# A planned RWKV-7 + MLP kernel on one core: whole instruction orders compared by four timing cases and a stateful TensorE clock

## Chip, core and metric

The kernel runs on one NeuronCore of one Trainium2 chip. The metric is device time in microseconds (us) of one launch, all inputs and outputs in the chip's memory. Before the change it took 732.19, 736.9 and 741.88 us in three runs; the median is 736.9 us.

## What is computed

An RWKV-7 recurrence for 4 batches x 8 heads over 768 tokens with head size 40, then a two-layer MLP with SiLU (320 to 2048 to 320) on the 3072 resulting rows. Everything is float32.

```
for t in range(768):                       # per batch and head, state is 40 x 40
    y[t]  = r[t] @ state
    Sa    = state @ a[t]
    state = state * w[t][None, :] - outer(Sa, b[t])
    state = state + outer(v[t], k[t])
x   = y as rows (3072, 320)
h   = x @ w_in                             # 320 -> 2048
out = (h * sigmoid(h)) @ w_out             # 2048 -> 320
```

## The kernel before

The sequence is cut into 12 chunks of 64 tokens (`NN` = 12, `C` = 64); a chunk holds all 32 batch-head problems. Within a chunk the recurrence becomes matrix algebra. Each chunk n passes these stages, each a few calls of `add(engine, cost, do, reads, writes, priority, ...)`:

- `load`, `load_r`: DMAs of w, b, a, k, v (L565, L575) and r, v transposed (L592, L601).
- `prepare`: running products of w on VectorE (two scans, L627 and L645), scaled copies of k, b and a (L664, L654), then products of the scaled rows on TensorE (L682), a mask on VectorE (L729), the product with v (L744) and transposes (L769).
- `special` (chunks 0 to 2) and `inverse` (then every two chunks together, five times): the inverse of a triangular block for each problem. Substitution steps run on VectorE as a multiply and a reduction (L795, L796); `special` finishes with three corrections on TensorE and an add on VectorE (L958, L973). `merge` puts the halves of an inverse together with 32 x 32 matmuls (L1039, L1068) and copies between (L405 on ScalarE, L409 on VectorE; `ZQ` and `X` are the tiles).
- `chain`: the state G goes from chunk to chunk: L1111 (old state), a VectorE add (L1121), L1135 (solve) with copies of the result (`vu`, L407 and L411), L1166 (solve, transposed), L1223 (update), a VectorE add and scale into G (L1239), and the transpose of G (L1196).
- `read`: the outputs: L1269 (look), VectorE masks (L1281), L1308 (old state) and L1323 (write), VectorE scaling (L1334), stores to `xh` in memory (L1353). Chunk 0 goes straight to `xt` by DMAs (L1378); `bring` loads `xt` for the others (L1393, L1395).
- `moe`: the MLP for the chunk's 256 rows: L1405 and L1418 multiply `xt` by w_in (two of three row blocks, then the half block), ScalarE applies SiLU (L1428), L1445 multiplies by w_out, VectorE copies to `ot` (L1457), and a DMA stores it (L1460).
- `weights`: w_in and w_out arrive as 64-bit words and are turned into float32 on VectorE and ScalarE (L484 to L500). For the first three of nine units the sum of two halves is done on TensorE as a product with the identity (L508, 128 x 512) and the result multiplied in on VectorE (L520).

TensorE's steps thus come in two sorts: large ones of 8 to 32 instructions with long rows (L1405, L1418, L1445, L508), and small ones with 64 to 128 instructions of 32 to 64 columns each.

No engine's order is written by hand. `Plan.add` only records a step with its engine, a declared cost, its reads and writes and a priority; `k` is its number of TensorE instructions and `shape` a letter for its kind (F, R, T, Q, H, S). There are 383 steps on TensorE. `Plan.order` then makes one order for all engines, greedily: it keeps a time for each engine, and takes among the ready steps of an engine the one that starts earliest, with `URGE` times the priority added. For TensorE it adds what `turn` says for a change of kind (the tables `LEAVE` and `ENTER`) and what `walk` says for instruction blocks of 256. PSUM pairs and two SBUF tiles are given out on the way (`Room`).

`Plan.best` calls `order` 410 times. Ten draws have other urges; then 400 steps shift the priorities of one group of steps by up to 8 and keep the shift if the value is not larger. The value of an order is the sum over `CASES` of what `Plan.through` returns, which runs the finished order once more with fixed times. In `through` each TensorE instruction block is fetched at some pace after the block before it, plus `crowd` if DMA queues are busy; each hop between engines costs `hop`; DMAs move at `rate`; VectorE's costs are multiplied by `slower`. TensorE's clock is modelled in windows of 3.41 us:

```
SLOW = 2.8, 1.7
CASES = (1.0, 300.0, 0.15, 1.0), (1.5, 240.0, 0.15, 1.0), (1.5, 240.0, 0.25, 1.04)
WINDOW, FEW = 3.41, 0.42
...
pace = 0.5 if t > 30 and work.get(w - 1, 0.0) < few * width else 1.0
```

The kept order is issued as it stands, engine by engine. Nothing of `through` runs on the chip; it only chooses.

After the planned part comes a check of the running products and, if they left their range, a slow path under `tc.If` that is not taken with these inputs.

## Time and profile before

| | |
|---|---|
| median of 3 runs | 736.9 us |
| profiled execution | 742.53 us |
| its span, first to last instruction | 740.8 us |
| mean granted TensorE clock | 0.976 |
| TensorE busy in 0 to 60 us | 27.5 us |
| TensorE busy in 60 to 140 us | 71.5 us |
| TensorE busy in 140 to 360 us | 209.1 us |
| TensorE busy in 360 to 580 us | 214.8 us |
| TensorE busy in 580 to 740.8 us | 151.7 us |
| VectorE busy in 60 to 140 us | 65.8 us |
| HBM traffic | 60.29 MB read, 14.61 MB written |

The busy shares are of the span. A TensorE row of the timeline merges equal matmuls that follow each other; each float32 matmul of the program stands as two matmuls and two weight loads. A row's bracket gives the idle time of the engine just before it and what ended it. "issue" means that the engine waited for nothing that the profile shows. The granted clock is a mean over a stretch, so 0.5 is a stretch wholly at half clock. The span is 1.7 us shorter than the execution's own time, which includes what lies before the first and after the last instruction.

### The profile page before, as it was taken

How to read it: one execution, taken by the hardware profiler on the slowest of the kernel's cores; microseconds unless marked ns; L12 is line 12 of the kernel's file. 1: busy time of each engine (PE TensorE's matmuls, PEld its weight loads, DVE VectorE, ACT ScalarE, POOL GpSimd, SP SyncE). 2: the span in 40 equal slices, each digit the busy share in tenths (PEclk: the TensorE clock that was granted, in tenths of full speed). 3: DMA queues.
4: the chain of work that ended last, by engine and by line, in shares of the span. 5: the costliest groups of instructions: out<-in, count | busy, mean ns of one | idle time of the engine just before them, and what ended most of it. 6: DMA issues, size and time to landing. Idle time of an engine off the chain costs nothing.

```text
span 740.8 us, 27279 instructions
## 1 busy us (share of the span) xinstructions
PE 674.7 (91%) x12666; PEld 540.5 (73%) x12666; DVE 419.5 (57%) x614; ACT 194.6 (26%) x241; POOL 14.3 (2%) x31
## 2 busy tenths in 40 slices
PE   2179799898899999999999999899999999999995
PEld 2176577678678677878778878778777778788773
DVE  6845799976479256299273397362686449321000
ACT  3251635523212411404304205124114211202020
POOL 2300000000000000000000000000000000000000
PEclk9996999999999999999999999999998999999998
DMA  7770654742632453525353506333233321401000
GB/s 248 160 227 11 195 210 126 222 116 47 161 107 58 96 135 98 139 61 125 112 133 106 161 19 144 95 99 92 73 93 81 97 60 32 126 21 41 18 1 22
DMA packets 117979, 77.15 MB, mean 104 GB/s; under 512 B 65506, under 2 KB 114338, under 8 KB 117218
## 3 DMA queue, kind: packets, MB, share of 16 engines
q1 hardware_dynamic: 113352, 64.54, 32.9%
q0 software_dynamic: 2096, 10.49, 4.3%
q8 instruction: 101, 1.65, 0.9%
q10 hardware_dynamic: 2410, 0.30, 0.3%
q14 instruction: 20, 0.16, 0.1%
HBM read 60.29 MB, written 14.61 MB: 101 GB/s over the span
## 4 chain that ended last, share of the span: by engine, by line
PE 80%; DVE 8%; DMA 3%; ACT 3%; issue 3%; SPq 1%; ACTq 1%; DVEq 0%
PE pair L1445 27%; PE pair L1405 21%; PE pair L1418 5%; PE pair L1269 4%; PE pair L682 3%; PE pair L1323 3%; PE pair L958 2%; PE pair L1135 2%; PE pair L1223 2%; PE pair L1068 1%; PE pair L1166 1%; PE pair L508 1%; PE pair L744 1%; PE pair L1308 1%; PE pair L1111 1%
## 5 line engine op out<-in xcount | busy, mean ns | idle before, releaser
L1445 PE MATMUL pair<-wo,gts 128*128 128x320 f32 x768 | 219.8, 442 | 1.1 <-issue 1.1
L1445 PEld LDWEIGHTS pair<-wo,gts 128*128 128x128 f32 x768 | 144.7, 192 | 60.4 <-issue 4.3
L1405 PE MATMUL pair<-xt,wi 128*128 128x256 f32 x768 | 175.5, 386 | 1.6 <-ACT R L756 1.3
L1405 PEld LDWEIGHTS pair<-xt,wi 128*128 128x128 f32 x768 | 145.7, 192 | 24.5 <-ACT R L756 1.4
L1428 ACT ACTIVATE gts<-pair 128x1024 f32<-128x1024 f32 x48 | 46.5, 1020 | 134.5 <-PE pair L1418 108.3
L682 PE MATMUL pair<-a,kb 40*64 40x64 f32 x1536 | 32.2, 236 | 35.8 <-DVE a L654 28.7
L1457 DVE COPY ot<-pair 128x320 f32<-128x320 f32 x24 | 11.8, 490 | 92.4 <-PE pair L1445 88.9
L796 DVE TENSOR_REDUCE XI<-XI 128x64 f32<-128x512 f32 (+9 forms) x85 | 58.6, 690 | 2.9
L682 PEld LDWEIGHTS pair<-a,kb 40*64 40x64 f32 x1536 | 28.6, 149 | 38.5 <-issue 20.5
L1418 PE MATMUL pair<-xt,wi 64*128 64x256 f32 x384 | 47.9, 389 | 0.0
L1281 DVE TENSOR_TENSOR lam<-pair,ml 128x1024 f32<-128x1024 f32 x22 | 26.4, 1220 | 32.9 <-PE pair L1269 30.4
L1418 PEld LDWEIGHTS pair<-xt,wi 64*128 64x128 f32 x384 | 35.1, 187 | 6.7 <-issue 2.6
L795 DVE TENSOR_TENSOR XI<-XI,mi 128x1024 f32<-128x1024 f32 (+8 forms) x60 | 33.6, 559 | 9.6 <-DMA mi<-md 8.3
L1334 DVE TENSOR_TENSOR lam<-pair,wz 128x1024 f32<-128x1024 f32 x11 | 13.5, 1223 | 38.8 <-PE pair L1323 38.8
L1269 PEld LDWEIGHTS pair<-r,vut 40*64 40x64 f32 x1536 | 25.9, 142 | 6.8 <-issue 5.9
L664 DVE TENSOR_TENSOR kb<-kbv 128x512 f32<-128x512 f32 (+1 forms) x36 | 29.7, 861 | 0.3
L1269 PE MATMUL pair<-r,vut 40*64 40x64 f32 x1536 | 28.5, 228 | 1.2 <-issue 1.2
L627 DVE TENSOR_TENSOR_SCAN kbv<-wz,zt 128x1024 f32<-128x1024 f32 x12 | 27.5, 2291 | 0.5
L645 DVE TENSOR_TENSOR_SCAN wz<-wz,zt 128x1024 f32<-128x1024 f32 x12 | 27.5, 2289 | 0.3
L756 ACT COPY R<-pair 128x640 f32<-128x640 f32 x12 | 8.3, 693 | 67.1 <-PE pair L744 61.5
L795 DVE TENSOR_TENSOR XI<-XI,xs 128x1024 f32<-128x1024 f32 (+1 forms) x25 | 25.3, 1010 | 0.8
L407 ACT ACTIVATE vu<-pair 64x640 f32<-64x640 f32 x13 | 9.1, 698 | 60.3 <-PE pair L1135 59.4
(151 smaller groups left out, 687.7 us busy)
## 6 DMA issues: line engine op xcount, KB each, us to landing
wz<-in_wT SPq DMA_DIRECT2D x12, 512.0 KB
kbv<-in_bT SPq DMA_DIRECT2D x12, 512.0 KB
a<-in_aT SPq DMA_DIRECT2D x12, 512.0 KB
kbv<-in_kT SPq DMA_DIRECT2D x12, 512.0 KB
r<-in_rT SPq DMA_DIRECT2D x48, 96.0 KB
vut<-in_vT SPq DMA_DIRECT2D x48, 96.0 KB
vu<-in_v SPq DMA_DIRECT2D x24, 160.0 KB
out<-ot SPq DMA_DIRECT2D x48, 80.0 KB
```

Source lines behind the costliest of these rows:

```text
L627: nc.vector.tensor_tensor_scan(back(V), back(W[:, 2 : 2 + Q * C]), zt, 1.0, ALU.mult, ALU.add)
L645: nc.vector.tensor_tensor_scan(Z, Z, zt, 0.0, ALU.mult, ALU.add)
L664: TTn[engine].tensor_tensor(out=at_(kb, place(is_b, first), (576 * step, 4 // step), (128, 4), (1, C)), in0=blocks((kf, bf)[is_b]), in1=bl ...
L682: nc.tensor.matmul(room.tile[half(b), j, g * C : g * C + C], lhsT=kb[rows(j), place(is_b, q) : place(is_b, q) + C], rhs=A[rows(j), q * C : ...
L795: nc.vector.tensor_tensor(out=at_(tmp, 0, *dims), in0=x, in1=y, op=ALU.mult)
L796: nc.vector.tensor_reduce(out=out_, in_=at_(tmp, 0, *dims), axis=AX.X, op=ALU.add)
L1269: nc.tensor.matmul(pl.tile[half(1 - b if role else b), b, c * C : c * C + C], lhsT=vut[rows(b), role, hu, :], rhs=rs[rows(b), hh, :], star ...
L1281: lambda pl=pl, la=la: nc.vector.tensor_tensor(out=la.tile.rearrange("p (q t) -> p q t", q=Q), in0=pl.tile.rearrange("p a b -> p (a b)").r ...
L1405: nc.tensor.matmul(rooms[g].tile[:, f // 2, (f % 2) * T : (f % 2) * T + T], lhsT=wi[:, k, (4 * g + f) * 128 : (4 * g + f) * 128 + 128], rh ...
L1418: nc.tensor.matmul(rooms[g].tile[:, h, (f % 2) * T : (f % 2) * T + T], lhsT=wi3[half(h), g * 256 + (f % 2) * 128 : g * 256 + (f % 2) * 128 ...
L1428: nc.scalar.activation(out=gts[:, 4 * g * T : 4 * g * T + 4 * T], in_=rooms[g].tile.rearrange("p a b -> p (a b)"), func=AF.Silu)
L1445: nc.tensor.matmul(po[b].tile[:, 0, 0:DM], lhsT=g4[:, f, 128 * b : 128 * b + 128], rhs=wo[:, f, :], start=f == 0, stop=f == NF - 1,)
```

## The change

It touches only the figure by which `best` compares orders, and the two tables that `turn` reads get a letter L that no step has. The number of cases goes from three to four, and each case now carries its own two times for instruction blocks in place of the pair `SLOW`. The clock of `through` is no longer worked out from the window before alone: it has a state, which begins at half. A window without work in the one before puts it at half; at full it stays full if the window before held at least 0.38 of its width in work, at half it rises if that was at least 0.48. Work at half clock now counts half.

```diff
-    LEAVE = {"F": 0.09, "R": 0.2, "T": 0.13, "Q": 0.13, "H": 0.12, "S": 0.11}
-    ENTER = {"F": 0.08, "R": 0.1, "T": 0.03, "Q": 0.03, "H": 0.03, "S": 0.03}
+    LEAVE = {"F": 0.09, "R": 0.2, "T": 0.13, "Q": 0.13, "H": 0.12, "S": 0.11, "L": 0.13}
+    ENTER = {"F": 0.08, "R": 0.1, "T": 0.03, "Q": 0.03, "H": 0.03, "S": 0.03, "L": 0.03}
...
-    SLOW = 2.8, 1.7
-    CASES = (1.0, 300.0, 0.15, 1.0), (1.5, 240.0, 0.15, 1.0), (1.5, 240.0, 0.25, 1.04)
-    WINDOW, FEW = 3.41, 0.42
-
-    def through(self, out, crowd, rate, hop, slower):
+    CASES = (
+        (2.0, 1.9, 3.0, 300.0, 0.35, 1.0),
+        (2.6, 1.3, 1.5, 240.0, 0.25, 1.0),
+        (2.0, 1.9, 1.5, 240.0, 0.25, 1.05),
+        (2.6, 1.9, 0.0, 300.0, 0.25, 1.05),
+    )
+    WINDOW, FEW = 3.41, (0.38, 0.48)
+
+    def through(self, out, before, after, crowd, rate, hop, slower):
...
-        fetched, count, shape, work = [0.0, 0.0], 0, "Q", {}
-        before, after = self.SLOW
+        fetched, count, shape = [0.0, 0.0], 0, "Q"
+        window, work, pace = -1, 0.0, 0.5
...
-                        pace = 0.5 if t > 30 and work.get(w - 1, 0.0) < few * width else 1.0
+                        if w > window:
+                            known = w == window + 1 and work >= few[pace < 1.0] * width
+                            window, work, pace = w, 0.0, 1.0 if known else 0.5
                         d = min((w + 1) * width - t + 1e-9, left / pace)
-                        work[w] = work.get(w, 0.0) + d
+                        work += d * pace
```

## Prediction

> **What bounds the kernel now.** I read the page first (busy shares, slices, chain of waits), then TensorE alone: its timeline with the idle time before each group[...].

> ```profile
> PE 674.7 (91%) x12666; PEld 540.5 (73%) x12666; DVE 419.5 (57%) x614; ACT 194.6 (26%) x241; POOL 14.3 (2%) x31
> ...
> PE   2179799898899999999999999899999999999995
> ...
> PEclk9996999999999999999999999999998999999998
> ...
> PE 80%; DVE 8%; DMA 3%; ACT 3%; issue 3%; SPq 1%; ACTq 1%; DVEq 0%
> ```

> TensorE is 91% busy and is 80% of the chain that ended last. It is empty only in the first slices; elsewhere it waits in small pieces. Its work is fixed: the change adds no matmul and takes none away. So only three things can move: idle time, time at half clock, and the cost of changing from one kind of step to another.

> Next, TensorE in stretches of 3.41 us. Columns: stretch, its length, TensorE busy (matmuls), granted clock, DMA share, GB/s.

> ```profile
> 49.79:53.20 3.41, 0.65 (x36) 1.00 0.36 49
> 53.20:56.61 3.41, 3.41 (x116) 0.50 0.17 43
> 56.61:60.02 3.41, 3.41 (x53) 0.50 0.02 5
> 60.02:63.43 3.41, 3.41 (x97) 0.50 0.02 5
> 63.43:66.84 3.41, 3.41 (x16) 0.50 0.00 0
> 66.84:70.25 3.41, 3.41 (x124) 1.00 0.02 5
> 70.25:73.66 3.41, 3.07 (x129) 1.00 0.11 38
> 73.66:77.07 3.41, 1.67 (x80) 1.00 0.29 86
> 77.07:80.48 3.41, 3.24 (x8) 0.51 0.74 211
> ```

> A stretch with little work is followed by one at half clock, which loses 1.7 us. The clock comes back after a stretch full of work, but not after every one: the two from 56.61 and 60.02 were full (small matmuls and some L508) and it stayed at half; after the one from 63.43, mostly L508, it rose.

> Last, the timeline of TensorE, with idle time and its releaser in brackets, and two rows of VectorE's:

> ```profile
> 74.24 0.60 PE L1196 MATMUL pair<-ident,G 40*104 40x40 f32 x16 [0.92 <-DVE G L1239]
> 77.24 5.33 PE L1405 MATMUL pair<-xt,wi 128*128 128x256 f32 x16 [1.32 <-ACT R L756]
> 198.79 0.69 PE L682 MATMUL pair<-a,kb 40*64 40x64 f32 x31 [2.77 <-issue]
> 564.16 1.22 PE L1068 MATMUL pair<-X,ZQ 32*32 32x32 f32 x64 [1.29 <-DVE ZQ L409]
> ```
> ```profile
> 560.93 2.29 DVE L645 TENSOR_TENSOR_SCAN wz<-wz,zt 128x1024 f32<-128x1024 f32 x1
> ...
> 563.41 0.70 DVE L409 COPY ZQ<-pair 32x512 f32<-32x512 f32 x1
> ```

> There are two kinds of wait: for a result of VectorE or a DMA, and "issue", where TensorE has its operands but no instruction to start. After 60 us the timeline's idle entries add up to 26 us, 10.3 of them issue. Half clock after 60 us (two stretches to 66.84, one at 77, one at 200, one at 247, two at 565 to 572) costs 7 x 1.7 = 12 us. So **38 us**, 5% of the span, is all that an order can win there.

> [...] half clock ran from 53.2 to 66.8 us, four windows. [...] The trace has 101 packets and 1.65 MB on the instruction queue, 16 KB each[...].

> **The change part by part.** All operations, their dependences and declared costs stay. Only the figure by which whole orders are compared changes, and so which order is kept. The new letter L in LEAVE and ENTER belongs to no step: nothing. I compared the instruction orders of the two built programs. Of 383 TensorE steps 126 have the same place, 232 lie within one place and 294 within two. Up to 62.5 us every engine does the same: 0, and the start-up wait and the half clock from 53 us stay.

> (a) *62 to 83 us.* One L508 pair (1.9 us at half clock) leaves the place ahead of L1323 and goes between L1223 and L1196. There it fills the 0.92 us wait for G. L1323 ends 1.9 us earlier, so the copies into xt, which ended the 1.32 us before L1405, go out earlier too; and with both gone the window from 73.66 would hold enough and 77.07 be at full clock (1.7). Together -3.9. The danger: the window from 63.43 now holds 1 us of L508 and 2.4 of L1323. If that isn't enough, half clock lasts until L1405, through 7.4 us of small steps and the two L508 pairs among them, at twice that time: +7.4, less the gaps and the half window above, is +3.5. I take the gain[...]. VectorE is 19 us of 20 busy from 100 to 140 with the conversion of weights, and absorbs part: half of it: **-2.0** (-3.9 to +3.5).

> (b) *83 to 141 us.* Two L958 now follow each other and wait for the L973 add (1.22 us and handover: +1.5). One L508 goes ahead of the first L958, whose wait of 1.24 shrinks by 1. L1166 now follows L1135, so its 1.62 goes, and L1223 waits some 0.6 for two copies of 0.7 on ScalarE. The sum is about -0.5 and lies beside full VectorE: 0. On SP, eight ms stores (5.15 us of issuing at 125.5) and the xs load move behind the r and vut loads and the xh stores. So L1308 no longer waits 0.84 and 0.91 at 139 us for r: **-1.7** (-1.7 to 0). The ms stores now stand between the first xt load and the other two, 5 us later for these; L1405 wants xt at 154 where it came by 142, so it is covered; that cover gone, the 5 us would show. xs comes later than VectorE's steps at 144 us use it, perhaps, but VectorE idles 2.5 us just after. On POOL the weight load into XI goes ahead of two others. It waited for L958 until 102.4 us and they went at 100.7 and 101.2: under 2 us, hidden behind VectorE's queue.

> (c) *The inverse at 524 to 564 us.* ZQ's copy stood in VectorE's order behind the inverse, L627, three L664 and L645; TensorE waited 1.29 and 0.38 us and then ran two windows at half clock (3.4). In the new order L627 stands ahead of the inverse, a second L1405/L1418 group and eight L1445 ahead of L1039, so from the inverse's start TensorE has L1445 13.1, L1405 14.0, L1418 3.9 and small steps 2.8: 33.8 us. VectorE has the inverse 24.0 (the 30.1 from 524.1 to 554.2, less 3.9 of other rows and 2.3 idle), two ot copies 1.0, L664 2.4, L645 2.3, L654 1.2 and small ones 0.9: 31.8. Waits gone, with 2 us to spare: **-5.1** (-5.1 to 0). Late next is the same copy.

> (d) *Issue.* Each small step is 64 to 128 instructions, a matmul and its weight load each. In runs of small steps between large ones (L1405, L1418, L1445, L508) I count what exceeds 320: 3936 before, 4672 after; runs of 512 or more: 8 before, 12 after. Without the first run, before 60 us, and another that both have, 2144 against 2880. The 10.3 us over 2144 is 4.8 ns each; 736 more: **+3.5** (0 to +7).

> (e) *Changes of kind.* 231 before, 246 after. L1445 x8 alone takes 2.35 us, x64 in one piece 17.42, or 2.18 for eight: 0.17 for a change in and out, 0.09 each. 15 more: **+1.3** (0 to +2.5).

> Sum: -2.0 -1.7 -5.1 +3.5 +1.3 = **-4.0 us**. The profiled execution took 742.5 us (span 740.8), so 738.5 on its scale; it stands 5.6 above the median of 736.9, so **733** in the median.

> **The rivals.** *Nothing in effect:* both orders come from the same start by the same kind of small shifts, so gains and losses cancel: 737. For it: the places above. Against: SP, POOL and VectorE queues do differ.

> *Faster:* the new clock rule finds places for small steps so that few windows fall short; half of the 38 us goes: 737 - 19 = 718. For it: (a), (b) and (c) all go that way. Against: other waits, such as 2.77 at 196 and 0.7 to 0.9 elsewhere, stand at places where the order is hardly changed.

> *Slower:* the longer runs of small steps run dry. At 196 us a run of 384 instructions met a DMA share of 0.85 to 1.08 and cost 2.77 and then half a window, 1.7: 4.5. Four more runs of 512 at that price are 18: 755. It decides only where the run meets such DMA traffic; after 580 us, at a share of 0.18, no issue wait shows, which speaks against all four doing so.

> **How the numbers follow.** Forecast 0.37, nothing 0.16 (these two are "same"), faster 0.31, slower 0.16. About 2%, 15 us, is what a measurement of this kernel can tell from no change. The forecast's own bounds, -10.7 to +13 if all ends meet, make 726 to 750. Eight in ten reaches to the middle of both other cases and a little past: 712 to 753.

> **What would show it.** (a) window from 66.84 at full clock and no wait before L1196; (b) no r wait before the second L1308; (c) full clock after the fifth inverse and L1068 without a wait; (d) issue idle after 60 us near 14 us, from 10.3. If half clock lasts from 53 to beyond 70 us, (a) has the wrong sign; if issue waits reach 20 us, the slower rival holds.

## The result and the profile after

| | before | after | ratio, 95% interval |
|---|---|---|---|
| median, first comparison | 739.89 us (21 runs) | 745.14 us (21 runs) | 1.0081 [1.0052, 1.011] |
| median, second comparison (after_again) | 738.69 us (51 runs) | 742.15 us (14 runs) | 1.0033 [0.9998, 1.0068] |
| profiled execution (span) | 742.53 us (740.8) | 742.0 us (740.1) | |

The medians are of all executions, while the ratios leave out those more than 1.5% above the fastest of their kernel, so the two need not agree. The change makes the kernel slower, by 0.3 to 0.8%: 5.2 us in the first comparison, 3.5 in the second, whose interval just takes in 1. I had forecast 4 us less. The executions of one kernel lie some 14 us apart (before: 732.19 to 746.07; one execution of after stands alone at 988.34). The profiled one of before is 2.6 us above its median, that of after 3.1 below, so the pair, equal within a microsecond, doesn't show the loss. It does show what moved.

The page of the kernel after, the lines that were shown of before:

```profile
PE 673.1 (91%) x12666; PEld 538.9 (73%) x12666; DVE 420.5 (57%) x614; ACT 194.3 (26%) x241; POOL 13.1 (2%) x31
...
PE   2189879998899999999998999999999899999995
...
PEclk9997999999989999999999999999999999999998
...
PE 86%; DVE 6%; issue 3%; DMA 2%; ACT 2%; SPq 0%; ACTq 0%; DVEq 0%
```

The same work and nearly the same busy time; the chain holds more TensorE (86% for 80%) and less of VectorE, DMA and ScalarE. So operand waits (waits for another engine or a DMA) did become fewer. After 62 us the timeline's operand waits add up to 9.6 us (15.7 before), its issue waits to 17.7 (10.3 before). Half clock while TensorE was busy cost 13.1 us after 50 us (15.1 before), and 1.7 of that difference lies before 72 us, where executions of one order differ too (last section). The three pieces, +7.4, -6.1 and -2.0, make -0.7, as the spans do. What the order won at operands it gave back at issue.

In both profiles the granted clock is 1.0 or 0.5, and from 43 to 736 us its changes lie 3.41 us or a whole multiple of that apart: half clock lasts 3.41, 6.83, 10.24 (after) or 13.65 us (before), full clock 10.24 to 525.65. A window is from here on a stretch of 3.41 us. After in such stretches (stretch, length, TensorE busy, weight loads, VectorE, ScalarE, GpSimd, granted clock, DMA share, GB/s):

```profile
60.02:63.43 3.41, 3.41 (x54) 1.79 (x49) 2.85 (x6) 0.00 (x0) 0.00 (x0) 0.50 0.02 5
63.43:66.84 3.41, 3.41 (x129) 3.05 (x126) 1.75 (x6) 0.39 (x1) 0.00 (x0) 0.99 0.00 0
...
73.66:77.07 3.41, 3.05 (x7) 2.52 (x8) 3.04 (x4) 1.25 (x3) 0.00 (x0) 0.51 0.77 211
```
```profile
101.15:104.56 3.41, 2.44 (x132) 2.12 (x123) 3.31 (x7) 2.42 (x3) 0.70 (x2) 1.00 1.00 394
104.56:107.97 3.41, 2.29 (x128) 2.19 (x128) 2.10 (x5) 0.00 (x0) 0.00 (x0) 0.98 1.01 413
107.97:111.38 3.41, 0.50 (x16) 0.30 (x8) 1.59 (x2) 1.15 (x1) 0.00 (x0) 0.50 0.38 127
111.38:114.79 3.41, 3.41 (x16) 2.69 (x9) 3.12 (x4) 0.00 (x0) 0.00 (x0) 0.51 0.38 100
```

The first fence is the stage of step (a): full clock from 63.43, and the half-clock stretch that stood at 77 is now at 73.66. The second is new. Between 101 and 111 us TensorE is busy for 5.2 of 10.2 us, in the first two stretches beside DMAs at full share. The third and the fourth are at half clock. In the timeline of the same place (start, length, line and tiles, count, idle before):

```profile
101.81 1.10 PE L1173 MATMUL pair<-X,R 64*40 64x64 f32 x64 [0.52 <-DVE wi L527]
102.84 1.27 PE L1230 MATMUL pair<-vu,kt 128*40 128x40 f32 x56
105.68 0.35 PE L1230 MATMUL pair<-vu,kt 128*40 128x40 f32 x8 [1.56 <-issue]
105.96 2.19 PE L1276 MATMUL pair<-r,vut 40*64 40x64 f32 x120
111.05 0.49 PE L1276 MATMUL pair<-r,vut 40*64 40x64 f32 x8 [2.91 <-issue]
111.47 5.29 PE L1412 MATMUL pair<-xt,wi 128*128 128x256 f32 x16
```

Line numbers of the kernel after are 7 higher. L1142, L1173, L1230 and two L1276 now follow each other: 640 instructions in one run, where before stood two large steps between them. It stops twice **in the middle of a row of equal matmuls**, with 8 of 64 left. Between the two stops lie 8 + 120 = 128 matmuls, with their weight loads 256 instructions. They ran in 2.5 us; the end of the second stop lies 5.4 us after that of the first.

Before, at the same place:

```profile
102.06 3.72 PE L1405 MATMUL pair<-xt,wi 128*128 128x256 f32 x16
105.72 1.14 PE L1135 MATMUL pair<-R,X 64*64 64x40 f32 x64
106.79 2.00 PE L1418 MATMUL pair<-xt,wi 64*128 64x256 f32 x16
```

The two large steps have 16 matmuls each in 3.7 and 2.0 us: few instructions in a long time, and no issue wait shows up to 117 us.

The DMA queues of the kernel after, two quarters of a microsecond (103.25 to 103.5 and 108.5 to 108.75; packets, MB, share of 16 engines):

```profile
q0 software_dynamic: 18, 0.08, 98.5%
q8 instruction: 1, 0.02, 24.0%
...
q8 instruction: 1, 0.02, 24.1%
q0 software_dynamic: 6, 0.02, 23.9%
```

These are the only two packets of the instruction queue from 102 to 112 us. Each lies 2.2 to 2.55 us ahead of the end of an issue wait (105.68, 111.05), and they are 5.25 us apart. The queue (q8) moved 101 packets in the launch, 1.65 MB, and 2 x 12666 instructions of TensorE are 99 times 256. In the profiles of before and after 26 issue waits of more than 0.3 us lie after 62 us; from one to the next TensorE starts 255 to 4096 instructions, in all 24 cases a multiple of 256 to within one. So I take this queue to feed TensorE, 256 instructions with each packet. The other traffic is the weights on the software queue (q0). So it is elsewhere: the waits of after that end at 398.18 and 402.11 have packets at 395.75 and 399.75 (each within a quarter of a microsecond), those at 469.81 and 473.28 at 467.25 and 470.75. In the 18 profiles of this document every issue wait of more than 0.3 us after 62 us, 205 in all, ended 2.1 to 3.2 us after the last packet of this queue, where packets are 7 us apart on average. So an issue wait here is **a block of 256 instructions that comes late**. The 14 such waits of after make 17.5 of its 17.7 us.

### The profile page after: what moved, and what is told of

Read it like the earlier page. It is cut to its first block, busy times and chain, and to the rows that moved or that the text cites. A ratio compares the mean times of both kernels' runs of the same rounds, so it can differ in the third digit from the quotient of the medians.

```text
span 740.1 us, 27291 instructions
## 1 busy us (share of the span) xinstructions
PE 673.1 (91%) x12666; PEld 538.9 (73%) x12666; DVE 420.5 (57%) x614; ACT 194.3 (26%) x241; POOL 13.1 (2%) x31
## 3 DMA queue, kind: packets, MB, share of 16 engines
q8 instruction: 101, 1.65, 0.9%
## 4 chain that ended last, share of the span: by engine, by line
PE 86%; DVE 6%; issue 3%; DMA 2%; ACT 2%; SPq 0%; ACTq 0%; DVEq 0%
PE pair L1452 29%; PE pair L1412 23%; PE pair L1425 6%; PE pair L1276 4%; PE pair L689 3%; PE pair L1330 3%; PE pair L965 3%; PE pair L1230 2%; PE pair L776 2%; PE pair L1142 1%; PE pair L751 1%; PE pair L1075 1%; PE pair L1315 1%; PE pair L1118 1%; PE pair L1173 1%
## 5 line engine op out<-in xcount | busy, mean ns | idle before, releaser
L1452 PE MATMUL pair<-wo,gts 128*128 128x320 f32 x768 | 219.6, 441 | 1.4 <-issue 1.4
L1452 PEld LDWEIGHTS pair<-wo,gts 128*128 128x128 f32 x768 | 144.2, 192 | 60.6 <-issue 4.7
L1412 PE MATMUL pair<-xt,wi 128*128 128x256 f32 x768 | 176.6, 387 | 1.3 <-ACT R L763 1.3
L1412 PEld LDWEIGHTS pair<-xt,wi 128*128 128x128 f32 x768 | 145.9, 193 | 24.2 <-ACT R L763 1.5
L1276 PEld LDWEIGHTS pair<-r,vut 40*64 40x64 f32 x1536 | 26.3, 142 | 11.7 <-issue 10.6
L1276 PE MATMUL pair<-r,vut 40*64 40x64 f32 x1536 | 29.7, 229 | 4.9 <-issue 4.9
L763 ACT COPY R<-pair 128x640 f32<-128x640 f32 x12 | 8.3, 695 | 95.8 <-PE pair L751 90.4
L1008 ACT COPY mi<-XI 128x1024 f32<-128x1024 f32 x5 | 10.1, 2015 | 60.6 <-DVE XI L803 60.6
```

Of the source, the lines that this page charges most:

```text
L1276: nc.tensor.matmul(pl.tile[half(1 - b if role else b), b, c * C : c * C + C], lhsT=vut[rows(b), role, hu, :], rhs=rs[rows(b), hh, :], star ...
L1412: nc.tensor.matmul(rooms[g].tile[:, f // 2, (f % 2) * T : (f % 2) * T + T], lhsT=wi[:, k, (4 * g + f) * 128 : (4 * g + f) * 128 + 128], rh ...
L1452: nc.tensor.matmul(po[b].tile[:, 0, 0:DM], lhsT=g4[:, f, 128 * b : 128 * b + 128], rhs=wo[:, f, :], start=f == 0, stop=f == NF - 1,)
```

## The experiments

All kernels below compute everything, with the same steps; only orders differ. "Beyond 320" is the count of step (d). A "run" is from here on an unbroken run of small TensorE steps. The half-clock loss is the sum of (1 - granted clock) x length over stretches of 3.41 us from 50 to 728 us; where TensorE stands idle in such a stretch, that time is in both columns. They are of one profiled execution, which can lie some microseconds from the median: clock_only's 6.8 above, s_late's 9.0 and a_mid_moved's 8.1 below. A median is of 6 to 22 executions. Numbers of lines differ by what the edit adds.

| kernel | beyond 320 | median; that of before beside it | ratio, 95% interval | issue idle after 62 us | half-clock loss |
|---|---|---|---|---|---|
| before | 3936 | | 1 | 10.3 | 15.4 |
| after | 4672 | 745.14, 739.89 | 1.0081 [1.0052, 1.011] | 17.7 | 15.4 |
| after_again | 4672 | 742.15, 738.69 | 1.0033 [0.9998, 1.0068] | 16.2 | 18.8 |
| b_long | 6240 | 763.47, 740.31 | 1.0307 [1.0247, 1.0368] | 22.7 | 32.4 |
| b_short | 3360 | 740.18, 740.31 | 0.997 [0.9934, 1.0006] | 9.0 | 13.6 |
| times_only | 3776 | 736.93, 740.31 | 0.9964 [0.9936, 0.9992] | 7.8 | 5.4 |
| clock_only | 4384 | 748.88, 740.31 | 1.0119 [1.0063, 1.0175] | 14.5 | 27.3 |
| b_seed2 | 4736 | 747.33, 738.96 | 1.0145 [1.0087, 1.0203] | 12.4 | 17.1 |
| a_moved | 3584 | 741.29, 738.96 | 1.0048 [1.0018, 1.0078] | 15.9 | 11.1 |
| b_moved | 5184 | 748.27, 738.96 | 1.0142 [1.0084, 1.0199] | 12.4 | 20.8 |
| a_short | 3584 | 732.38, 738.96 | 0.9931 [0.9905, 0.9956] | 9.5 | 8.8 |
| a_short2 | 3008 | 734.09, 740.13 | 0.9958 [0.9917, 0.9998] | 7.9 | 4.8 |
| s_early | 4160 | 743.85, 740.13 | 1.0102 [1.0034, 1.017] | 15.1 | 20.5 |
| s_late | 4448 | 740.73, 740.13 | 1.0025 [0.9991, 1.0058] | 10.5 | 8.2 |
| s_late_moved | 3360 | 735.8, 740.13 | 0.9975 [0.9926, 1.0023] | 9.7 | 3.9 |
| a_mid | 4352 | 740.49, 738.69 | 1.0007 [0.9975, 1.004] | 11.1 | 13.8 |
| b_mid | 4256 | 743.45, 738.69 | 1.0057 [1.0028, 1.0086] | 14.2 | 12.0 |
| a_mid_moved | 3264 | 741.47, 738.69 | 1.002 [0.9984, 1.0057] | 7.3 | 5.3 |

The theory ("runs"): TensorE runs out of instructions in long runs of small steps, and the waits then bring stretches at half clock. Rivals: that either half of the change is itself harmful; that it is the chance of the search which order comes out; that other things of the orders decide and the count only goes with them.

### Run length as a term of the figure

The value of an order gets a term for run length: -0.03 x long in the kernel before (b_long), +0.03 (b_short). The kinds F and R are the large steps; they end a run.

```diff
+            run, long = 0, 0
+            for op in out:
+                if op["engine"] == "PE":
+                    run = 0 if op["shape"] in "FR" else run + op["k"]
+                    long += min(op["k"], max(0, run - 320))
-            return sum(spans), out, {i: room.slot for i, room in rooms.items()}
+            return sum(spans) + -0.03 * long, out, {i: room.slot for i, room in rooms.items()}
```

> The kernel before with one term in the compared figure that rewards instructions beyond 320 in an unbroken run of small TensorE steps: 6240 such instructions, from 3936 (after the change: 4672); changes of kind 239, from 231. Theory of runs (TensorE runs out of instructions in long runs of small steps, and the gap also costs half-clock windows): after the change 736 more cost about 6 us, 8 ns each, so 2304 more cost 11 us (at the 4.8 ns of the prediction) to 18 us; issue waits after 60 us near 21 us or more. Theory of the draw (each order that the search keeps is a chance one, and its time scatters whatever the runs): within 7 us of the kernel before, either way, issue waits near 10.

> The kernel before with the opposite term: 3360 instructions beyond 320, runs of 512 or more 5 in place of 8, changes of kind 249, from 231. Theory of runs: 576 fewer, 3 to 5 us faster, less up to 2 us for 18 changes of kind; issue waits after 60 us near 7 us. Theory of the draw: anywhere within 7 us.

b_long is 23.2 us slower for 2304 instructions more: 10 ns each, twice the price of step (d). Some of its stops, from the timeline:

```profile
465.69 1.13 PE L687 MATMUL pair<-a,kb 40*64 40x64 f32 x31 [2.06 <-issue]
469.75 0.65 PE L1044 MATMUL pair<-ZQ,sb 32*32 32x32 f32 x32 [0.76 <-issue]
...
521.76 1.16 PE L1228 MATMUL pair<-vu,kt 128*40 128x40 f32 x50 [0.55 <-issue]
525.47 1.03 PE L1274 MATMUL pair<-r,vut 40*64 40x64 f32 x52 [1.24 <-issue]
```

They stand in the midst of steps again (31, 32, 50 and 52 of 64 left), in pairs 4.1 and 3.7 us apart. Issue idle rises by 12.4 us and the half-clock loss by 17.0, of which 15.3 fell while TensorE was busy; operand waits fall by 4.7, and b_long's own span is 24.4 longer (765.2). The larger part of the price is at half clock, behind the waits. b_short missed: 576 fewer should have won 3 to 5 us, and it is not told apart from before. Fewer instructions beyond 320 did not win by themselves.

### The two halves of the change, and another draw

times_only takes the new cases and block times with the old clock; clock_only the new clock with the old cases; b_seed2 is the kernel before with another start of its search. The search draws at random from a fixed start, and the one order that it keeps is called a draw below. The edits are shown against the kernel before:

```diff
 times_only
+        (2.0, 1.9, 3.0, 300.0, 0.35, 1.0),
...
+    def through(self, out, before, after, crowd, rate, hop, slower):
 clock_only
+    CASES = (2.8, 1.7, 1.0, 300.0, 0.15, 1.0), (2.8, 1.7, 1.5, 240.0, 0.15, 1.0), (2.8, 1.7, 1.5, 240.0, 0.25, 1.04)
...
+    WINDOW, FEW = 3.41, (0.38, 0.48)
 b_seed2
-        rng = Random(1)
+        rng = Random(2)
```

> The four new cases with their block times, the clock of before. 3776 instructions beyond 320, changes of kind 240. Theory of runs: as before, -1 to 0 us, since the runs are not longer. If the new block times are what harms (they make long runs look cheap): about +6 us as with the whole change. Theory of the draw: within 7 us either way.

> The new clock with state, the three cases and the block times of before. 4384 instructions beyond 320, changes of kind 239. Theory of runs: 448 more, +2 to +4 us. If the new clock is what harms: about +6 us. If the new block times are what harms: 0. Theory of the draw: within 7 us either way.

> The kernel before with another seed of the search: 4736 instructions beyond 320, 11 runs of 512 or more. Its figure is that of before. Theory of runs, with the run length a matter of the draw: 6 to 8 us above before. If the new figure is what harms: 0 to 2 us from before.

The new cases with their block times alone give an order 3.4 us faster, the clock alone one 8.6 us slower, where the theory of runs had 2 to 4; its interval overlaps that of the whole change. But b_seed2 keeps the old figure and is 8.4 us slower, with 4736 beyond 320, about as many as after has. So what one draw of the search gives varies by at least as much as the change does. From a single draw of each half it can't be said that the new clock rule is worse. Both the old figure and the new clock rule let long runs through.

### The changed figure with the term

a_short is the kernel after with + 0.04 x long, a_short2 with + 0.08.

```diff
...
-            return sum(spans), out, {i: room.slot for i, room in rooms.items()}
+            return sum(spans) + 0.04 * long, out, {i: room.slot for i, room in rooms.items()}
```

> The change with a term in the compared figure that adds for instructions beyond 320 in a run: 3584. Theory of runs: the new cases and clock harm only through the runs, so 2 to 4 us below before. If the new figure harms in another way (waits or half clock elsewhere): some 6 us above before. Theory of the draw: within 7 us either way.

> As a_short with double weight on the term: 3008 instructions beyond 320, the run of 992 near 165 us cut to 736, changes of kind 250. Theory of runs: 5 to 9 us below before (a_short with 3584: 5 us below). If further shortening wins nothing, as its waits moved to operands: within 3 us of before.

a_short is the best order found: 0.9931 [0.9905, 0.9956], faster than both kernels. At the place of the stops it has large steps:

```profile
99.34 1.14 PE L1147 MATMUL pair<-R,X 64*64 64x40 f32 x64
100.42 2.00 PE L1430 MATMUL pair<-xt,wi 64*128 64x256 f32 x16
102.34 1.43 PE L1235 MATMUL pair<-vu,kt 128*40 128x40 f32 x64
```

No issue wait follows up to 116 us, and the clock is full from 101 to 115. Doubling the weight of the term wins nothing more. Each of the two is again one draw; that both are faster than before speaks against the changed figure doing harm by itself.

### A few large steps moved by hand

The draw is taken out of the question: an order as kept, with only five large steps moved by a few TensorE steps, the other engines' orders as they were, PSUM pairs given anew. a_moved breaks later runs of after (two L1452 and three L1412 moved in); b_moved makes runs in the kernel before (four L1445 and one L1405 moved out). The moves shown are those of a_moved:

```diff
+    MOVES = (401, 533), (816, 965), (600, 737), (1140, 1236), (1027, 1083)
...
+        for n, m in self.MOVES:
+            op = self.ops[n]
+            out.remove(op)
+            out.insert(out.index(self.ops[m]), op)
...
```

> The order of after with five large steps of TensorE (two of L1452, three of L1412) each moved two to four TensorE steps earlier, into a run of small steps; every other engine's order is as in after. 3584 instructions beyond 320 (after: 4672, before: 3936). Theory of runs: after lies some 6 us above before; 1088 fewer at 8 to 10 ns are 9 to 11 us, less about 1 us for more changes of kind, so 2 to 4 us below before, and issue waits after 60 us near 9 us in place of 17.7. If after's time has another cause (the order of VectorE or of the DMAs, the start of a stage): still about 6 us above before.

> The order of before with five large steps of TensorE (four of L1445, one of L1405) each moved a few TensorE steps, out of a run of small steps; all other engines as in before. 5184 instructions beyond 320, from 3936. Theory of runs: 1248 more, +10 to +12 us, and issue waits near 19 us in place of 10.3. If runs are not the cause: within 3 us of before, as these steps' operands are there long before.

b_moved costs 9.3 us for 1248 instructions more, at least what the change cost. But the way there is not the one forecast: its issue waits are 12.4 us, where near 19 were expected, while operand waits rose too (18.2 us for 15.8), and the windows at half clock at 129 and 132 us stand behind such. a_moved missed: it should have come out 2 to 4 us below before, with issue waits near 9 us, and is 2.3 us above it with 15.9, not told apart from after by its interval. It has fewer beyond 320 than before has, but leaves the run at 100 us alone, and its profile still has 1.66 and 3.53 us of issue there. The count is not the whole; that place matters is the reading tried next.

### Early part and late part

Both orders have done the same 447 steps by the third L1135 (L1142) after 60 us, at about 181 us; counted from 0, it is that of chunk 2. s_early is after's order up to there and before's from there; s_late the reverse; s_late_moved is s_late with the five moves of a_moved.

```diff
+    FIRST = [
...
+        out = [self.ops[n] for n in self.FIRST] + [op for op in out if op["n"] not in set(self.FIRST)]
...
```

> All engines in the order of after for the first 91 TensorE steps (to the second chunk's L1135, some 181 us), then in the order of before; at that place both orders have done the same steps. 4160 instructions beyond 320 (before 3936, after 4672). If the place decides (the new run of 640 at 102 to 111 us meets full DMA queues and cost 4.5 us of issue wait and two windows at half clock, 7.9 us, against some 5 us of waits that the new order saves up to 181 us): +2 to +6 us. If the count alone decides: +2 us, and the larger part of the loss in the other half.

> The other way about: the order of before for the first 91 TensorE steps, then that of after. 4448 instructions beyond 320. If the place decides: -2 to +2 us, as the later long runs meet less DMA traffic and the fifth inverse no longer stalls. If the count alone decides: 512 more at 8 to 10 ns, +4 to +5 us.

> As s_late, with the five large steps moved into runs as in a_moved: 3360 instructions beyond 320. Theory of runs: faster than s_late by 2.4 us (what the five moves gave in after) to 9 us (count times 8 ns), so below before by 2 to 7 us. If runs are not the cause: as s_late.

The early part of the change alone costs 3.7 us in the medians, about as much as the whole (six executions; the interval of the ratio is wide, 1.0034 to 1.017). The late part alone costs 0.6, not told apart from none, and with its runs broken it is 4.3 us under before, though the interval just takes in 1.

### The stretch from 95 to 181 us

b_mid keeps before's order for the first 46 TensorE steps (to about 95 us), then takes after's up to the border at 181 us, on all engines: of the change it has the run of 640 and whatever else moved between 95 and 181 us. a_mid is the mirror: after without that stretch, and so without that run. a_mid_moved adds the five moves, and after_again is after once more beside them. The edit is that of the splice, with another list.

> The changed kernel's order for the first 46 TensorE steps (to about 95 us), then the order of the kernel before up to the second chunk's L1142 (about 181 us; by there both have done the same 447 steps), then the changed kernel's again. It takes away the run of 640 small TensorE instructions at 100 to 111 us (there are 256, 256, 352 and 384 in its place) and nothing later; instructions beyond 320 in a run go from 4672 to 4352. Theory, long runs under transfers: no issue wait of over 1 us between 95 and 115 us, no half-clock windows there, and 4 to 8 us less than the changed kernel: a ratio of 0.997 to 1.003 to the kernel before. Rival, that the first 95 us or the operand waits and VectorE's order there cost what the early part costs: as the changed kernel, 1.006 to 1.010.

> The mirror: the order of the kernel before for its first 46 TensorE steps, then the changed kernel's up to about 181 us, then again that of the kernel before. It brings the run of 640 into the kernel before and nothing else of the change (instructions beyond 320: 3936 to 4256). Theory: two issue waits of together 3 to 5 us near 105 and 111 us, half-clock windows after them, a ratio of 1.005 to 1.011. Rival (first 95 us): 0.998 to 1.002.

> The first of these with five large steps moved two to four TensorE steps into later runs, as was done alone at 1.0048: 3264 instructions beyond 320. If the early run and the later ones add up: 0.991 to 0.998, below the kernel before. If the early run is not the cause: 1.003 to 1.006, as the moves alone gave.

> The changed kernel once more, on the chip and in the rounds of the three above: a ratio of 1.005 to 1.011, and a second profile. Theory: issue waits of over 1 us at about 105 and 111 us again in the same instructions, and the whole of issue idle after 62 us within 15 to 20 us; if those waits are a matter of one execution, they lie elsewhere or are under 2 us together.

b_mid, timeline:

```profile
105.24 0.35 PE L1266 MATMUL pair<-vu,kt 128*40 128x40 f32 x8 [0.74 <-issue]
105.52 2.11 PE L1312 MATMUL pair<-r,vut 40*64 40x64 f32 x120
110.61 0.49 PE L1312 MATMUL pair<-r,vut 40*64 40x64 f32 x8 [2.98 <-issue]
```

and after_again:

```profile
107.23 0.35 PE L1230 MATMUL pair<-vu,kt 128*40 128x40 f32 x8 [1.49 <-issue]
...
113.15 0.49 PE L1276 MATMUL pair<-r,vut 40*64 40x64 f32 x8 [3.53 <-issue]
```

The same two stops, before the same matmuls, 3.7 and 5.0 us; s_early has them too (1.50, 2.80). They belong to the order, not to one execution. (The ratio of after_again, 1.0033, fell short of the 1.005 expected.) Brought into the kernel before, this stretch costs 4.8 us (1.0057, above 1 with its interval): about as much as the change. The rival, that the first 95 us do it, gave 0.998 to 1.002 for b_mid and falls. But the run did not come alone. The splice at 95 us makes two L1001 (L958 of before) follow each other, the second of them waits for VectorE, and a window at half clock follows from 96.1 us:

```profile
95.00 2.80 PE L1001 MATMUL pair<-XI 64*64 64x64 f32 x64 [2.22 <-DVE XI L1016]
```

So the 4.8 us are the price of the stretch; how much of them is the run's is not shown.

The mirror is weaker. a_mid is level with before, 1.7 us under after_again, where 4 to 8 were expected, and the intervals of these two overlap. As expected no stop is left at 95 to 115 us. In its place stands one new stop, in the product with the old state, and a stretch at half clock after it:

```profile
138.59 0.60 PE L1358 MATMUL pair<-r,GT 40*40 40x64 f32 x26 [3.00 <-issue]
```

By the profiles the run is not needed for the loss. From the first L958 after 60 us to the third L1135 (the same steps in each order) it takes 88.4 us in before and 90.3 in s_late, which has the same order there, 94.9 in after and 95.8 in b_mid, and in a_mid, without the run, 94.9 as well. (One execution each.)

a_mid_moved missed: 0.991 to 0.998 were expected, and it is 1.002. Its profile has the fewest issue waits of all (7.3 us), but is of an execution 8.1 us under the median. The same moves won 4.9 us on s_late. So gains don't add up, and what takes them back there stays open.

Over all 18 rows a straight line through time against the count has a slope of 7.6 ns for each instruction beyond 320 and a correlation of 0.88, with 3.2 us of scatter about it (a_short 5.1 below, a_mid_moved 6.7 above). Without b_long, which lies far out, it is 6.1 ns and 0.77. So the time goes with run length, but the orders share most of their places and do not count as independent; orders with equal counts still differ by 1%.

The mean granted clock of every execution is on record too. Taken as (1 - clock) x span and averaged over all executions of a kernel and of before beside it, half clock makes 2.1 us of the 3.5 that after_again loses, 7.1 of 9.2 in b_moved and 14.3 of 21.4 in b_long, but 2.7 of 5.2 in b_mid and only 2.5 of 8.8 in b_seed2 (each good to about 1 us). So half clock is often the larger part of the loss, and not always.

## Why the prediction was wrong

It had the change 4.0 us faster; it is 3.5 to 5.2 us slower. (Some 3 us of the absolute time's error are the base: three runs gave 736.9 us for the kernel before, more runs 739.) Point by point, from the profile of after:

- **(a) 62 to 83 us, -2.0: right in part.** The wait before L1203 is gone, and full clock came from 63.43, a window earlier than I said. The window ahead of it held 2.07 us of L515; but that of before from 56.61 held 2.07 us of L508 and half clock stayed, so what raised it is not shown. And L1412 at 74.02 still waits 1.34 us, and its window is at half clock as before: both only moved from 77. I had put this wait down to the copies into `xt`. The line names ScalarE's copy R (L756, L763 after), which starts only once six issues of these copies, 5.6 us, have left ScalarE's queue, in both kernels. So of the 3.9 allowed for, the order won the 0.9; the window gained at 63.43 is another than the one that I counted on, and not the order's alone, for the start-up clock differs between executions (below).
- **(b) 83 to 141 us, -1.7: a line misread.** Of the two waits that I put down to r only the first was for r; the second was already an issue wait. So 0.8 was to be won, not 1.7. The wait for r is gone, an issue wait of 1.21 stands where one of 0.91 stood, and about 0.5 is left (first fence: before; second: after):

```profile
138.86 0.66 PE L1308 MATMUL pair<-r,GT 40*40 40x64 f32 x32 [0.84 <-DMA r<-in_rT]
140.43 0.60 PE L1308 MATMUL pair<-r,GT 40*40 40x64 f32 x26 [0.91 <-issue]
```
```profile
137.31 0.38 PE L1315 MATMUL pair<-r,GT 40*40 40x64 f32 x10 [1.21 <-issue]
```

  The pair of L965 waits 1.40 us, as forecast (1.5). The rest of the stage I put at nothing, "beside full VectorE", and there the new run of 640 lies.
- **(c) the fifth inverse, -5.1: right.** On VectorE ZQ's copy waits 0.61 us for its product, no longer behind a scan (first fence: VectorE's timeline), and TensorE's wait of 1.29 is 0.41 (second: TensorE's); from 561 to 575 us the clock is full:

```profile
572.68 0.70 DVE L416 COPY ZQ<-pair 32x512 f32<-32x512 f32 x1 [0.61 <-PE pair L1046]
```
```profile
574.04 1.20 PE L1075 MATMUL pair<-X,ZQ 32*32 32x32 f32 x64 [0.41 <-ACT ZQ L412]
```

  The waits were 1.67 together and half clock 3.4: 4.7 gained.
- **(d) issue, +3.5: the step that failed.** The mechanism was right, the term too small: issue idle rose by 7.4 us (5.9 in the second profile), and I put the half clock behind such waits at nothing. I spread the price evenly, a mean over runs of which most meet little DMA traffic. The two stops at 100 us alone make 4.5 us, where the sum had 1.5 (320 instructions beyond 320 at 4.8 ns). They stand beside the weights' transfers at 394 and 413 GB/s and just behind them, and their blocks come 5.25 us apart, against 3.5 and 4.0 us at 470 us and 400 us of the launch, where the DMA share is 0.02 and 0.04. Two windows at half clock follow, as two follow the waits at 201 and 206. TensorE was busy for some 3.9 us of their 6.8, so they cost 2.0 us more, together 6.5. (The 7.9 in the expectation of s_early counts their idle time twice.) Over all executions half clock makes 2.1 of the 3.5 us lost. I had the very case in the rival "slower" (2.77 us and half a window at a share of 0.85 to 1.08) and didn't ask which of the new runs would meet such a share. Its own bound, 20 us of issue idle, was not reached, so that rival at 755 didn't hold either. That the run at 100 us is what makes the change slow is not shown: a_mid, without it, stops elsewhere.
- **(e) changes of kind, +1.3:** not tried apart.

## What to carry to other kernels

Price a run of small matmuls by its place: count the instructions (weight loads too), and look at the DMA share where it will stand. A block of 256 instructions that TensorE worked off in 2.5 us came here every 3.2 to 6.0 us where two in a row were waited for (47 times), so keep a large matmul step between small ones, above all beside bulk transfers, and charge the half-clock windows that can follow a stall, for the time in which TensorE is busy in them (in after two windows each at the stops of 100 us and the waits of 201 and 206, none at the 1.87 and 1.20 us of 398 and 402). A run broken in one place can bring the stop back in another, as in a_mid. Where a search picks the order, put that into its figure, and judge a change of the figure by more than one draw.
